# Folded-sum blocks as eight tiles, with gate and wide output products taken in column parts, in a Fourier-mixing and gated-feed-forward kernel

## The chip, the core and the metric

The kernel runs on one core of a Trainium2 chip. The metric is the device time of one execution in microseconds (us), the median of several runs. A core has a matrix engine (TensorE, in the profile PE, with its weight loads as PEld), three engines for elementwise work (VectorE or DVE, ScalarE or ACT, GpSimd or POOL), and SyncE (SP), which issues DMA transfers. TensorE writes to PSUM, eight banks of 512 float32 values for each of 128 partitions.

## The reference

```python
X = np.fft.fft(x, axis=1)          # x: (8, 3008, 256) float32
X = np.fft.fft(X, axis=2)
x = X.real.reshape(8 * 3008, 256)
gate = 1.0 / (1.0 + np.exp(-(x @ w_gate)))     # w_gate, w_val: (256, 1536)
val = x @ w_val
return gate * val @ w_out                      # w_out: (1536, 256)
```

Eight batches are transformed along the sequence and the features, the real part is kept, and each of the 24064 rows goes through a gated feed-forward layer.

## The kernel before, in words

Everything is float32. The symmetry of the transform lets the kernel compute sums over folded rows only, and the feature transform is merged into the gate and value weights (`merge`, line 411), so that three kinds of matrix products remain for each batch.

**The folded sums.** `quarter(b, blk)` (line 621) computes, for batch `b` from 1 to 7 and `blk` 1 then 0, a block of 48 products: 2 (`what`) x 2 (`part`) x 3 (`q`) x 4 (`TILES`, four groups of 32 partitions). Each has 31 or 32 contraction rows, 128 output columns of weights and 95 streamed columns, so it fills a quarter of the array's rows and the four of a round can run side by side, each into a PSUM bank of its own. Line 636 is the switch: for a (b, blk) in `HALVED` (line 78), each product is made as two, with 64 columns of weights each, so that eight tiles of 32 x 64 stand side by side. Before, seven of the fourteen blocks are in `HALVED`: (1, 0), (2, 0), (3, 1), (4, 1), (4, 0), (5, 0), (6, 1). Batch 0 is summed otherwise (`half`, line 596).

**The gate and value products.** The frequencies of a batch are cut into six chunks of 252 (the last of 246), and each chunk has 12 slices of 128 of the 1536 hidden features. An iteration `i` of the main loop (line 1153) is one such slice; there are 576, 72 to a batch. Its products are `front_a(i)` (two products, tile `pf` from `pk`) and `front_b(i)` (line 791; two products, `g` = 0 and 1, tile `pf` from `qk`), 252 columns each.

**The output products.** `back(p, part)` (line 859) multiplies the gated features by the output weights. From the second chunk on, an iteration makes 5 of the 15 products in `PRODUCTS` (line 67), 168 columns each. For the first chunk of batch 0 it takes the plain form of lines 866 to 882: two products of 504 columns for each of the 12 slices, 24 in all.

A float32 product is two passes of TensorE, and each pass is a weight load and a matmul: the page counts 12508 of each, and the program 6254 products. All products are issued through the helper `mm` at line 134, so all have that line in the profile; they are told apart by their tiles (`sum`, `pf`, `po`).

**The order of the work** is written out by hand. Each engine executes its instructions in the order in which the loop issues them. `mid` (line 1095 and line 1144) says in which iterations a block stands: block (b, blk) is issued in iteration (b - 1) x 72 + (4 - blk) x 12 + 5, and 12 later for b = 1, after that iteration's output products and before its `front_b`. Batches 2 to 7 issue transfers between partitions (`swap`, line 541) some iterations ahead of their blocks. ScalarE takes the four banks of a block away (line 646).

**The place of a block.** TensorE's instructions come to it by a DMA queue of their own, in packets of 16384 bytes. Over the program that is one packet for each 256 instructions. A block's place, in what follows, is the number of TensorE instructions ahead of it in the program, modulo 256, with four for each product and one for each separate wait. Before, the seven blocks in `HALVED` have the places 0, 248, 47, 228, 34, 215 and 14 (in order of time), the other seven 130, 122, 109, 89, 76, 195 and 65.

Of the kernel before, what the change touches and what calls it, by code (L numbers as in the profile page):

```python
# [74 lines left out]
          (12, 12, 11, 1), (13, 13, 6, 1), (7, 7, 10, 0), (5, 5, 7, 1))  # L75
C_LAST = (14, 9, 14, 0)
OUT = (3, 12)
HALVED = ((1, 0), (2, 0), (3, 1), (4, 1), (4, 0), (5, 0), (6, 1))
HUGE = float((2 ** 24 - 1 - 2 ** 20) * 2.0 ** -7)


# [1 line left out]
def kernel(  # L83
# [19 lines left out]
    NFT = F // P  # L103
# [28 lines left out]

    def mm(o, l, r, start, stop):
        nc.tensor.matmul(o, l, r, start=start, stop=stop, skip_group_check=True)  # L134

    def bank(name, other=None):
        if other is not None:
            return pso.tile([P, 512], F32, name=name, tag=f"po{other}")
        return psx.tile([P, 512], F32, name=name, tag="x")
# [43 lines left out]
    G2 = const.tile([P, 2, F], F32, name="G2")  # L183
# [227 lines left out]
    def merge(ws, g, c, other):  # L411
        cs = slice(c * WC, (c + 1) * WC)
        ps = bank("ps", other)
        for h in range(2):
            for t in range(2):
                mm(ps[:, h * WC : (h + 1) * WC], dt[:, t, h * HD : (h + 1) * HD], ws[:, t, :],
                   h == 0 and t == 0, t == 1)
        nc.scalar.copy(G2[:, g, cs], ps[:, WC : 2 * WC])
        nc.scalar.copy(G1[:, g, cs], ps[:, 0:WC])
        for f in range(c * WC // P, (c + 1) * WC // P):  # L420
            nc.sync.dma_start(
                out=ge[:, g, f : f + 1], in_=G2[0:1, g, f * P : (f + 1) * P])
# [173 lines left out]
    def half(b, w, d, blk, sn, other=None):  # L596


        c0, n = ((0, NE), (NE, NO))[blk]
        ev, od = [bank(name, other and other[i])[:, 0:n] for i, name in enumerate(("ev", "od"))]  # L600

        def sums(*qs):
            for q in sorted(qs, key=lambda q: q % 2):
                mm((ev, od)[q % 2], w(q), ST[int(sn)][0:NP, q, c0 : c0 + n], q < 2, q >= NQ - 2)

        def then():
            a = evp.tile([P, NE], F32, name="a", tag="a")[:, 0:n]
            nc.scalar.copy(a, ev)
            return lambda: places(d, blk, sn, a, od)
        return sums, then  # L610
# [10 lines left out]
    def quarter(b, blk):  # L621

        ps = [bank("sum", t + 1) for t in range(4)]
        for what in range(2):
            for part in range(2):
                for q in range(N3):
                    for t, (g, par, lo) in enumerate(TILES):
# [7 lines left out]
                        c0 = (2 * what + 1 - part) * NQ4  # L635
                        for at_ in (slice(0, HP), slice(HP, P)) if (b, blk) in HALVED else (slice(0, P),):
                            mm(ps[t][at_, c0 : c0 + NQ4], W[b, blk][what][rows, w, at_], tab,
# [111 lines left out]
    H, SF, EK = {}, {}, {}  # L749

    def cut(i):
        b, c, _ = groups[i // 3]
        k0, n = chunks[c]
        f = i % NFT
        return PQE[b], slice(k0, k0 + n), n, f, slice(f * P, (f + 1) * P)
# [8 lines left out]
    PF, AP, Z = {}, {}, {}  # L764
# [26 lines left out]
    def front_b(i):  # L791
        (_, qk, *_), ks, _, _, fs = cut(i)
        for g in range(2):
            mm(PF[i][:, g], G2[:, g, fs], qk[:, ks], False, True)

    def gate_a(i):

# [8 lines left out]
    def block(p, i):  # L806

        R = 2 * chunks[groups[p][1]][1] // 3
        return H[p][:, i % 3, i // 3 * R : (i // 3 + 1) * R] if i < 9 else SF[p][:, i - 9, 0:R]
# [19 lines left out]
    PO = []  # L829
# [3 lines left out]
    def rows_back(p, part):  # L833

        b, c, g = groups[p]
        k0, n = chunks[c]
        more = k0 + n > NK
        low, high = min(n, M - k0), n - more
        tiles = [(P, low - P, b * S + k0 + P), (n + more + P, high - P, b * S + S - k0 - n + 1 + more + P),
                 (0, P, b * S + k0), (n + more, P, b * S + S - k0 - n + 1 + more)]  # L840
        f0 = 3 * g + part
        if f0 == 0:
            PO[:] = [bank(f"po{t}", t) for t in range(4)]
            C[0] = cp.tile([P, 10 * WC], F32, name="c", tag="c")
        if g == NG - 1 and part < 2:
            return
        for t, (at_, m, r0) in enumerate(tiles):
            ps = PO[t][0:m, 0:D]
            for fh in (range(3) if g == NG - 1 else (part,)):
                f = 3 * g + fh  # L850
                mm(ps, H[p][:, fh, at_ : at_ + m], WL[0][:, f], f == 0, f == NFT - 1)
            if g == NG - 1:
                o = C[0][0:m, t * D : (t + 1) * D]
                (nc.vector.tensor_copy, nc.scalar.copy)[t % 2](o, ps)
                (nc.sync, nc.scalar)[t % 2].dma_start(out=out[r0 : r0 + m], in_=o)
        if part == 2:
            del H[p]

    def back(p, part):

        if p >= len(groups) - NG:
            return rows_back(p, part)
        b, c, g = groups[p]
        n = chunks[c][1]
        R = 2 * n // 3
        if p < NG:
            f = 3 * g + part
            if f == 0:
                PO[:] = [bank(f"po{t}", t) for t in range(2)]
            w = WO[f // 2].rearrange("p f (m h) -> p f h m", h=2)[:, f % 2]  # L870
            for h in range(2):
                mm(PO[h][:, 0 : 2 * n], w[:, h], H[p][:, part], f == 0, f == NFT - 1)
            if part == 2:
                del H[p]
            if f == NFT - 1:
                C[0] = cp.tile([P, 10 * WC], F32, name="c", tag="c")
                for x in OUT:
                    nc.gpsimd.memset(C[0][:, (x + 3) * R : (x + 3) * R + 40], 0.0)
                for h, copy in enumerate((nc.scalar.copy, nc.vector.tensor_copy)):
                    copy(C[0][:, OUT[h] * R : (OUT[h] + 3) * R], PO[h][:, 0 : 2 * n])  # L880
                finish(b, c, True)
            return
        if part == 0 and g == 0:
            PO[:] = [pso.tile([P, 2 * WC], F32, name=f"po{t}", tag=f"po{t}") for t in range(NB)]
        for at_, (hb, wb) in list(enumerate(PRODUCTS))[part * 5 : part * 5 + 5]:
            t, j = divmod(PLACE[at_], 3)
            mm(PO[t][:, j * R : (j + 1) * R], wf[:, g, wb], block(p, hb), g == 0 and at_ % 3 == 0,
               g == NG - 1)
            if g == NG - 1 and at_ % 3 == 2:
                if t == 0:  # L890
                    C[0] = cp.tile([P, 10 * WC], F32, name="c", tag="c")
                    nc.gpsimd.memset(C[0][:, 15 * R : 15 * R + 40], 0.0)
                (nc.vector.tensor_copy if t == 1 or t == 3 else nc.scalar.copy)(  # L893
                    C[0][:, 3 * t * R : 3 * (t + 1) * R], PO[t][:, 0 : 3 * R])
        if part == 2:
            del H[p], SF[p]
            if g == NG - 1:
                finish(b, c)
# [119 lines left out]

    per = NFT * len(chunks)
    side, mid, gap, spare = {}, {}, {}, {}  # L1020

    def at(i, *fs):
        side.setdefault(i, []).extend(fs)
# [129 lines left out]
    for i in range(count):  # L1153
# [11 lines left out]
        if i + 1 in mid:  # L1165
            back((i - 5) // 3, (i - 5) % 3)
        n = 3 if i >= count - 8 else 2 + (i % 2 and i not in (3 * i0 + 7, 3 * i0 + 9))
# [12 lines left out]
        if i >= 5 and i + 1 not in mid:  # L1180
            back((i - 5) // 3, (i - 5) % 3)
        merges = use.pop(i, [])
        for f in merges[0 : min(i, 1)]:
            f()
        front_b(i)
        for f in merges[min(i, 1) :]:
            f()
# [9 lines left out]
    for i in range(count, count + 5):  # L1197
        back((i - 5) // 3, (i - 5) % 3)
# [49 lines left out]
```

## Time and profile before

| | |
|---|---|
| median of 3 runs | 1907.24 us (1907.17 to 1909.02) |
| the profiled execution's own time | 1906.5 us |
| its span, first to last instruction | 1904.7 us |
| TensorE busy | 1894.5 us, 12508 passes |
| VectorE, ScalarE, GpSimd busy | 1518.6, 1353.0, 1544.1 us |
| granted TensorE clock | 1.00 throughout |

Busy time is the union of an engine's instructions. Matmuls overlap (a pass of 252 columns is shown as 376 ns long, while the next one starts 213 ns later), so what a pass costs is read from the distance between starts, not from its length. The chain of waits follows the work that ended last back from the end of the program: where it names an engine, shortening that engine's work there shortens the program, as long as nothing else comes to be last.

### The profile page before, as it was taken

Reading aid. Unit: us, or ns where it says so; the run is one execution under the profiler, and the core shown is the slowest. Engines: PE = TensorE matmul, PEld = TensorE weight load, DVE = VectorE, ACT = ScalarE, POOL = GpSimd, SP = SyncE. Lnnn points to the kernel's source line nnn. Section 1 sums busy time; section 2 is a strip of 40 time slices with the busy share of each in tenths; the row PEclk is TensorE's granted clock in tenths of the full one; section 3 lists DMA queues with packets and bytes.
Section 4 is the critical chain, followed back from the end, with each engine's and each line's share of the span. In section 5 each row is a group of like instructions: output and inputs, shape, how many; then the busy total and the mean of one; then the engine's idle time right before and its main releaser. Section 6 shows DMA issues by size and latency. Waiting matters only on the chain.

```text
span 1904.7 us, 37401 instructions
## 1 busy us (share of the span) xinstructions
PE 1894.5 (99%) x12508; PEld 1754.8 (92%) x12508; DVE 1518.6 (80%) x3375; ACT 1353.0 (71%) x3235; POOL 1544.1 (81%) x2733
## 2 busy tenths in 40 slices
PE   8999999999999999999999999999999999999999
PEld 5789999999999999999999999999999999999998
DVE  7678887878979778887788878887788777977775
ACT  4777777777777777777767777777777777777775
POOL 2389879987999879997799878999689986877770
PEclk9999999999999999999999999999999999999999
DMA  9346222212122121211211112112110110010001
GB/s 315 121 137 78 70 89 54 71 32 81 23 64 53 31 87 33 62 40 37 89 38 49 46 39 81 39 52 55 41 66 18 37 36 15 15 25 17 14 18 30
DMA packets 197338, 109.41 MB, mean 57 GB/s; under 512 B 134823, under 2 KB 188818, under 8 KB 195354
## 3 DMA queue, kind: packets, MB, share of 16 engines
q1 hardware_dynamic: 196568, 106.50, 21.1%
q8 instruction: 100, 1.64, 0.4%
q14 instruction: 92, 0.75, 0.1%
q10 hardware_dynamic: 546, 0.51, 0.1%
q0 software_dynamic: 32, 0.00, 0.0%
HBM read 71.24 MB, written 47.87 MB: 63 GB/s over the span
## 4 chain that ended last, share of the span: by engine, by line
PE 97%; POOL 1%; DMA 1%; DVE 0%; SPq 0%; ACT 0%; issue 0%; ACTq 0%; POOLq 0%
PE pf L134 51%; PE po L134 43%; PE sum L134 2%; PE ps L134 1%; POOL sf L826 1%; DMA st<-in_stab_dram 0%; DMA raw<-in_moe_w_val_dram 0%; PE od L134 0%; SPq L193 0%; POOL x L508 0%; SPq L376 0%; PE pe L134 0%; PE ev L134 0%; DVE c L910 0%; DVE z L804 0%
## 5 line engine op out<-in xcount | busy, mean ns | idle before, releaser
L826 POOL TENSOR_TENSOR sf<-h,sf 128x168 f32<-128x168 f32 (+1 forms) x1104 | 620.7, 582 | 76.0 <-DVE h L820 72.4
L826 POOL TENSOR_TENSOR sf<-h 128x168 f32<-128x168 f32 (+1 forms) x920 | 520.5, 585 | 160.1 <-DVE h L820 158.4
L134 PE MATMUL pf<-qk,G 128*128 128x252 f32 (+1 forms) x2304 | 583.5, 376 | 0.3 <-ACT ae L789 0.2
L134 PE MATMUL pf<-pk,G 128*128 128x252 f32 (+1 forms) x2304 | 582.9, 376 | 0.0
L774 ACT ACTIVATE pf<-ek,ge 128x252 f32<-128x252 f32 (+1 forms) x1142 | 538.2, 471 | 23.0 <-DMA ge<-G 3.2
L134 PE MATMUL po<-sf,wf 128*128 128x168 f32 (+1 forms) x2944 | 508.3, 305 | 0.0
L789 ACT ACTIVATE ae<-pf 128x504 f32<-128x504 f32 (+1 forms) x576 | 338.9, 588 | 218.1 <-PE pf L134 216.7
L134 PEld LDWEIGHTS pf<-pk,G 128*128 128x128 f32 x2304 | 435.8, 190 | 53.6 <-ACT pf L774 2.0
L134 PE MATMUL po<-h,wf 128*128 128x168 f32 (+2 forms) x2584 | 461.6, 307 | 0.0
L134 PEld LDWEIGHTS po<-sf,wf 128*128 128x128 f32 x2944 | 453.4, 190 | 8.0
L820 DVE TENSOR_TENSOR h<-pf,z 128x252 f32<-128x252 f32 (+1 forms) x576 | 240.4, 417 | 275.4 <-ACT pf L817 271.7
L804 DVE TENSOR_TENSOR z<-ae,pf 128x504 f32<-128x504 f32 (+1 forms) x576 | 384.5, 668 | 81.3 <-ACT h L803 77.3
L910 DVE TENSOR_TENSOR c<-c 128x168 f32<-128x168 f32 (+1 forms) x920 | 440.9, 503 | 3.3
L134 PEld LDWEIGHTS pf<-qk,G 128*128 128x128 f32 x2304 | 410.6, 190 | 31.6 <-issue 2.0
L134 PEld LDWEIGHTS po<-h,wf 128*128 128x128 f32 x2584 | 410.4, 190 | 18.1 <-issue 1.1
L803 ACT ACTIVATE h<-pf 128x252 f32<-128x252 f32 (+1 forms) x576 | 216.8, 376 | 146.4 <-PE pf L134 129.1
L817 ACT ACTIVATE pf<-z 128x252 f32<-128x252 f32 (+1 forms) x576 | 214.3, 372 | 119.0 <-DVE h L816 116.9
L816 DVE TENSOR_TENSOR h<-h,pf 128x252 f32<-128x252 f32 (+1 forms) x576 | 232.7, 404 | 0.0
L826 POOL TENSOR_TENSOR sf<-sf 128x168 f32<-128x168 f32 (+1 forms) x184 | 101.6, 552 | 14.4
L826 POOL TENSOR_TENSOR sf<-sf,h 128x168 f32<-128x168 f32 (+1 forms) x184 | 109.5, 595 | 0.0
L893 ACT COPY c<-po 128x504 f32<-128x504 f32 (+1 forms) x138 | 78.5, 569 | 0.0
L920 DVE STREAM_TRANSPOSE os<-c 128x256 f32<-128x256 f32 x188 | 76.5, 427 | 0.1
(158 smaller groups left out, 868.8 us busy)
## 6 DMA issues: line engine op xcount, KB each, us to landing
x<-xr SPq DMA_DIRECT2D x14, 1536.0 KB
out_dram<-os SPq DMA_DIRECT2D x376, 56.0 KB
xr<-in_xf_dram SPq DMA_DIRECT2D x105, 128.0 KB
x<-x SPq DMA_DIRECT2D x112, 96.0 KB
xr<-in_xf_dram SPq DMA_DIRECT2D x14, 384.0 KB
ek<-ed SPq DMA_DIRECT2D x40, 126.0 KB
out_dram<-os SPq DMA_DIRECT2D x288, 7.0 KB
xr<-in_xf_dram SPq DMA_DIRECT2D x21, 124.0 KB
```

What stands on the lines that cost most here:

```text
L134: nc.tensor.matmul(o, l, r, start=start, stop=stop, skip_group_check=True)
L774: nc.scalar.activation(PF[i][:, g], EK[i // NFT], AF.Copy, scale=ge[:, g, f : f + 1])
L789: nc.scalar.activation(AP[i], PF[i], AF.Copy, scale=2.0)
L803: nc.scalar.activation(H[p][:, fh, 0:n], PF[i][:, 0], AF.Sigmoid)
L804: nc.vector.tensor_tensor(z[:, :, ::-1], AP.pop(i), PF[i], op=ALU.subtract)
L816: nc.vector.tensor_tensor(h[:, fh, 0:n], h[:, fh, 0:n], pf[:, 1], op=ALU.mult)
L817: nc.scalar.activation(pf[:, 0], z[:, 0], AF.Sigmoid)
L820: nc.vector.tensor_tensor(h[:, fh, n:], pf[:, 0], z[:, 1], op=ALU.mult)
L826: nc.gpsimd.tensor_tensor(block(p, dst), block(p, a), block(p, b), op=(ALU.subtract, ALU.add)[op])
L893: (nc.vector.tensor_copy if t == 1 or t == 3 else nc.scalar.copy)(C[0][:, 3 * t * R : 3 * (t + 1) * R], PO[t][:, 0 : 3 * R])
L910: nc.vector.tensor_tensor(t[:, dst * R : (dst + 1) * R], *v, op=(ALU.subtract, ALU.add)[op])
L920: nc.vector.transpose(os_[0][0][:, s, 0:nb, h, :], t[:, c0 : c0 + nb * TB])
```

## The change

All fourteen blocks are put in `HALVED`. A new helper, `parts_mm`, makes a product as `n` products of adjoining columns, each with the same weights; only the first may start the accumulation in the bank. `front_b` uses it with two parts for its second product (`g` = 1) in 186 iterations: in the `n` iterations ahead of a block that `PARTED` names, for nine of the blocks. The 24 wide products of the first chunk are made in two parts of 252 columns, the last five in three parts of 168.

```diff
-HALVED = ((1, 0), (2, 0), (3, 1), (4, 1), (4, 0), (5, 0), (6, 1))
+HALVED = ((1, 1), (1, 0), (2, 1), (2, 0), (3, 1), (3, 0), (4, 1), (4, 0), (5, 1), (5, 0), (6, 1), (6, 0), (7, 1), (7, 0))
+PARTED = {(2, 1): 15, (2, 0): 1, (3, 1): 31, (3, 0): 1, (4, 1): 33, (4, 0): 1, (5, 1): 38, (6, 1): 31, (7, 1): 35}
+THIRDS = 5
...
+    def parts_mm(n, o, l, r, start, stop):
+
+        w = o.shape[1]
+        for k in range(n):
+            at_ = slice(k * w // n, (k + 1) * w // n)
+            mm(o[:, at_], l, r[:, at_], start and k == 0, stop)
...
     def front_b(i):
...
-            mm(PF[i][:, g], G2[:, g, fs], qk[:, ks], False, True)
+            parts_mm(2 if g and i in parted else 1, PF[i][:, g], G2[:, g, fs], qk[:, ks], False, True)
...
             for h in range(2):
-                mm(PO[h][:, 0 : 2 * n], w[:, h], H[p][:, part], f == 0, f == NFT - 1)
+                parts_mm(3 if 2 * f + h >= 2 * NFT - THIRDS else 2, PO[h][:, 0 : 2 * n], w[:, h], H[p][:, part],
+                         f == 0, f == NFT - 1)
...
+    parted = {(b - 1) * per + (4 - blk + (b == 1)) * NFT + 4 - k for (b, blk), n in PARTED.items() for k in range(n)}
+    assert len(parted) == sum(PARTED.values())
```

The program then has 6805 products in place of 6254: 336 more in the seven blocks, 186 more gate products and 29 more output products. The other engines have the same instructions in the same order. The places of the fourteen blocks become, in order of time, 246, 52, 233, 43, 220, 30, 215, 25, 229, 35, 212, 18, 211 and 17.

## The prediction

> **What bounds the kernel now.** I read the page's busy times and its chain of waits first, to see which engine a saving has to come from.
>
> ```profile
> PE 1894.5 (99%) x12508; PEld 1754.8 (92%) x12508; DVE 1518.6 (80%) x3375; ACT 1353.0 (71%) x3235; POOL 1544.1 (81%) x2733
> ...
> PE 97%; POOL 1%; DMA 1%; DVE 0%; SPq 0%; ACT 0%; issue 0%; ACTq 0%; POOLq 0%
> PE pf L134 51%; PE po L134 43%; PE sum L134 2%; PE ps L134 1%; POOL sf L826 1%; DMA st<-in_stab_dram 0%; DMA raw<-in_moe_w_val_dram 0%; PE od L134 0%; SPq L193 0%; POOL x L508 0%; SPq L376 0%; PE pe L134 0%; PE ev L134 0%; DVE c L910 0%; DVE z L804 0%
> ```
>
> TensorE is 97% of the chain, and the folded sums are only 2% of it. Busy time alone would not prove the bound, since passes overlap, so I also compared starts. The median distance between the starts of successive passes is 213 ns for 252 columns, 143 for 168, 139 for 164 and 423 for 504: within 0.7 ns, 0.833 ns a column and 3 ns a pass. Over the whole trace the distances exceed this line by 2.5 us in the first 48 us and by 0.6 us at most in any later slice of 48 us. So TensorE streams columns without a gap, and what is taken from it or added to it shows one to one in the end. After the first 33 us, most of which go to transfers, the chain leaves TensorE twice for longer than 0.2 us, at 318.9 to 351.8 us (GpSimd, VectorE) and at 1620.8 to 1625.5 us (ScalarE), but both detours begin at a TensorE pass, so a shift ahead of them is passed on.
>
> Next the chain in narrow windows, which gives the price of one block in each form. The columns are start, length and number of passes on the chain. A block of four tiles:
>
> ```profile
> 1603.52 1.70 PE pf L134 x8
> 1605.22 2.86 PE sum L134 x96
> 1608.09 1.62 PE po L134 x10
> ```
>
> and one of eight tiles, block (2, 0), with the dearest of its kind, (6, 1), behind it:
>
> ```profile
> 452.14 1.70 PE pf L134 x8
> 453.84 2.53 PE sum L134 x141
> 456.38 1.62 PE po L134 x10
> ```
>
> ```profile
> 1332.54 1.70 PE pf L134 x8
> 1334.24 2.63 PE sum L134 x151
> 1336.87 1.20 PE po L134 x7
> ```
>
> The neighbours cost the same in all three (eight gate passes 1.70), so the block's own length is the whole difference: 2.86 against 2.53 us. All seven four-tile blocks read 2.86. Of the seven eight-tile ones five read 2.53 or 2.54, (4, 1) reads 2.58 and (6, 1) 2.63.
>
> **The change part by part.**
>
> **Blocks as eight tiles.** Seven blocks go from 2.86 to 2.53: 7 x 0.33 = 2.3 us less. Each issues 48 products more, and nothing waits for them but ScalarE's four copies, as before. Bounds for a new eight-tile block are the rows 2.53 and 2.63: a gain of 1.6 to 2.3.
>
> One rule of the Trainium skill speaks against this step: "TensorEngine Tiling (Array Packing)", section Instruction Overhead, gives each matmul a floor of some 60 cycles however few its columns, and warns against tiling too finely. At 2.4 GHz that is an estimated 25 ns, so 192 passes would take 4.8 us and seven blocks would lose 14 us. The row above disagrees: 2.53 us over 192 passes is 13 ns each.
>
> **Their places.** The change's column parts move the blocks. Places that gave 2.53 or 2.54 before are 215, 248, 0, 34 and 47. The two dear blocks stood at 228 and 14, in between, so by these seven rows place alone does not order the lengths. What else differs is the DMA traffic (the last two columns are the share of the DMA engines and GB/s):
>
> ```profile
> 453.70:456.90 3.20, 2.60 (x192) 2.42 (x192) 0.62 (x3) 1.00 0.04 8
> 873.90:877.10 3.20, 2.65 (x192) 2.47 (x192) 0.64 (x4) 1.00 0.44 98
> 1334.10:1337.30 3.20, 2.70 (x192) 2.51 (x192) 0.59 (x3) 1.00 0.54 119
> ```
>
> The dear ones are (4, 1) at 0.44 and (6, 1) at 0.54; (3, 1) at 0.21 has 2.54, the rest at most 0.11. The new places, 211 to 246 and 17 to 52, lie inside or within five of the range tried. If place was the cause, 0.15 us come back; if it is DMA, (4, 1) and (6, 1) stay as they are and block (1, 1), with a share of 0.46 in the same view, comes out some 0.07 short of its 0.33. I take 0 here, with -0.15 to +0.1 as its bounds.
>
> **Wide output products.** A product is two passes. Two parts of 252 in place of 504 cost 2 x (2 x 213 - 423) = 6 ns, 19 times; three parts of 168 cost 2 x (3 x 143 - 423) = 12 ns, 5 times. Together 0.2 us more. Rows for both widths exist, and the chain is TensorE's there.
>
> **Gate products in parts.** This is the open price: no full-width pass of 126 columns is in the trace. By the line above it takes 105 + 3 = 108 ns, so a product costs 4 x 108 - 2 x 213 = 6 ns more, and 186 of them 1.1 us. That is the floor of a pass, so the lower bound, and it holds only if the weights of the next pass, 128 columns each time, are loaded in that time. The trace shows two rows that limit this from above. The narrowest full-width pass, 164 columns, starts every 139 ns, still on the line, so a load takes no longer; that gives 4 x 139 - 426 = 130 ns and 24 us. Nearer is the four-tile block: there a round of four tiles loads the same 128 columns and streams only 95, which by the line need 82 ns. It takes 2.86 us / 24 = 119 ns with both ends of the block counted, and 111.7 ns between rounds inside it, by the starts of its loads and passes. So loading 128 columns, not streaming, sets the pace there, at about 112 ns: 4 x 112 - 426 = 22 ns, 4.1 us in all. But in that block a load starts some 30 ns after the pass ahead of it, behind the other three tiles' passes. In full-width rows it starts 2 ns after. The first two loads of a tile stand 108 ns apart. I therefore take 108 for the load too, as the nearest row without that queue, and 1.1 us as the price.
>
> The Trainium skill has a figure for this: "TensorE: Matmul & The Clock Gate", section LDWEIGHTS, gives a load its number of columns divided by 1.2 in ns, 107 for 128. By it the load hides under the 108 by a hair and the sum is the same; the 112 of the block is 5 ns above it, and no run shows it for the full array.
>
> Nothing but TensorE's stream is touched: the other engines' order is unchanged, and the end of a gate product moves by nanoseconds. The instruction queue fetches some nine packets more (the page's 100 carry 1.64 MB at 0.4% of the DMA engines).
>
> **Sum**, against the profiled execution's own 1906.5 us: -2.3 + 0 + 0.2 + 1.1 = -1.0, so 1905.5. The median of the runs shown is 0.7 higher, 1907.24. On it the forecast is **1906.2 us**. A difference of 0.2%, 3.8 us, is about what a measurement of this kernel can tell from no change (its three runs span 1.9), so this is a forecast of no visible difference.
>
> **Rivals.**
>
> *Weight loads pace the parts, at the inner rate of the four-tile block.* At 112 ns the parts cost 4.1 instead of 1.1, the sum is +2.0 and the time 1909.2, still within 0.2%. For it: that block is paced by loads of this width. Against it: its queue of four tiles.
>
> *The same, dearer: slower than before.* With the whole 119 ns of the block's round, parts cost 4 x 119 - 426 = 50 ns, 9.3 us in all; the sum is +7.2 and the time 1914.4. The point from which it is slower by over 0.2% is (3.8 + 2.1) us / 186 = 32 ns a product, a pass of 114.4 ns. For it: nothing full-width in the trace is quicker than 139. Against it: 119 counts the block's ends.
>
> *Bad places.* All fourteen blocks at the dearest length seen: 14 x 2.63 = 36.8, against 7 x 2.86 + 5 x 2.53 + 2.58 + 2.63 = 37.9 now. The gain is 1.1, the sum +0.2, the time 1907.4. A place that costs more than seen needs 0.4 us a block to reach 0.2%.
>
> *The change does not do what it says*, new blocks staying at 2.86: 1908.5. Seven rows of exactly this kind of block speak against it.
>
> *All parts free and both dear blocks cured:* -2.3 - 0.15 + 0.2 = -2.3, and 1904.9; the line's 3 ns a pass speaks against it.
>
> **Chances.** Forecast 0.57, loads at 112 ns 0.17, dear loads 0.07, bad places 0.10, not as it says 0.02, parts free 0.07. Slower by over 0.2% is the dear loads plus a little for a place worse than any seen: 0.08. Faster by over 0.2% needs 3.8 us where all blocks together can give 2.5: 0.03. Within 0.2%: 0.89. The range for 8 in 10 takes in parts free, the forecast, bad places and loads at 112 ns: 1904.8 to 1909.2.
>
> **What the profile after would show.** In the chain, fourteen blocks at 2.53 to 2.63 and none at 2.86. In the timeline, gate groups of six passes ahead of a block, with the next group 0.86 us behind (0.87 if loads take 112 ns, 0.90 if 119). In the first chunk, wide groups 1.70 us apart where it was 1.69. I would be wrong if a part's second pass started later than 110 ns after its first, or if a new block showed a stall of tenths of a microsecond.

## The result and the profile after

The changed kernel takes 1913.01 us (median of 8 runs, 1911.59 to 1913.57), the kernel before on the same chip 1907.13: a ratio of 1.0029, with a 95% interval of 1.0019 to 1.0038. It is slower by 0.3%, outside the forecast range. The profiled execution takes 1913.41 us, 6.9 more than the one of before; the span grows by the same 6.9. The forecast sum was -1.0.

From the page of the kernel after (the first line is the span, then the busy times, the instruction queue and the chain of waits):

```profile
span 1911.6 us, 39593 instructions
...
PE 1897.3 (99%) x13610; PEld 1775.3 (93%) x13610; DVE 1524.3 (80%) x3375; ACT 1356.5 (71%) x3235; POOL 1545.2 (81%) x2733
...
q8 instruction: 109, 1.79, 0.4%
...
PE 96%; POOL 1%; DMA 1%; DVE 0%; ACT 0%; SPq 0%; issue 0%; ACTq 0%; POOLq 0%
```

TensorE still carries the chain, at full clock, with 1102 passes and 9 instruction packets more. Its busy time grew by only 2.8 us; in the other 4.1 us of the longer span the profile shows it idle, and the page's percentages hide that. So I compared, pass by pass, the distance from each start to the next start with that of before. The loss stands in few places:

| Part | forecast | measured (us) |
|---|---|---|
| 186 gate products in parts | +1.1 | +4.1 |
| fourteen blocks, first start to the start of the next work | -2.3 | +1.5 |
| other stops of TensorE: one of 0.89, 14 instructions behind block (1, 0), less small differences | 0 | +0.7 |
| wide output products | +0.2 | +0.1 |
| start of the program, end, small differences | 0 | +0.5 |

**The gate parts.** TensorE's timeline ahead of block (6, 1), with start, length as shown, and count of passes:

```profile
1335.39 1.59 PE L136 MATMUL po<-sf,wf 128*128 128x168 f32 x10
1336.81 1.03 PE L136 MATMUL pf<-qk,G 128*128 128x252 f32 x6
1337.68 0.59 PE L136 MATMUL pf<-pk,G 128*128 128x252 f32 x2
```

The row of six is two passes of 252 columns and four of 126 (the row names the form of its first). From its start to the next row's it takes 0.87 us, the figure that the prediction gave to loads at 112 ns. By starts, the first 126-column pass is followed after 107.5 ns, the other three after 111.7, and the 252-column pass behind them takes 216.7 instead of 212.5. With those 4.2 ns that is 446.8 against 425.0 ns for the product: 21.8 ns, 186 times.

**The blocks.** The chain of waits around block (2, 0), and then around block (6, 1):

```profile
453.27 1.72 PE pf L136 x10
455.00 2.53 PE sum L136 x136
457.53 1.48 PE po L136 x9
```

```profile
1336.98 1.72 PE pf L136 x10
1338.70 1.64 PE sum L136 x90
1340.33 1.05 issue
1341.38 1.20 PE sum L136 x62
1342.59 1.62 PE po L136 x10
```

In each of these rows the block stands ahead of its own iteration's output products, which follow it as `po`. Block (2, 0) has the price foreseen, 2.53 us, and so have eight others; (3, 1) has 2.54. Block (6, 1) is cut in two by a piece named "issue", time in which TensorE waited for nothing that the profile shows, and takes 3.89 us. (The piece counts from the end of a pass, which the profile models; from start to start the stop is 1.29 us.) Block (7, 1) takes 3.89 too, (4, 1) 3.55 and (1, 1) 2.76. The three long ones, (4, 1), (6, 1) and (7, 1), stop once, after 117, 119 and 119 of their 192 passes, and always at the same kind of instruction: number 194 modulo 256 in the program, counted as the places are. I take this to be where a new instruction packet begins, and call such a point a *packet boundary*.

The trace has the packets of TensorE's queue themselves, and the five blocks of the kernel after with places from 211 to 229 show what separates them (times from the block's first pass, in us; a stop is the distance between two starts):

```
block   place  packet starts  takes  block stops for  goes on at
(3, 1)  220    -3.34          1.51   -
(5, 1)  229    -2.83          1.22   -
(4, 1)  215    -0.24          1.19   0.95             2.40
(7, 1)  211    +0.02          1.43   1.29             2.75
(6, 1)  212    +0.50          0.94   1.29             2.75
```

Where the packet started late, the block stopped, and went on 1.3 to 1.5 us after the packet's end (start plus what it takes). The stop behind block (1, 0) ends in the same way, 1.46 us after the end of its packet, though the chain names ScalarE's copies there; the kernel before has the same copies and no stop. My theory from here: an eight-tile block issues 256 instructions in 1.7 us, and the next packet isn't there by then. The rival: the long blocks come from their batch or from the data traffic beside them, and the boundary is a coincidence; or, for the gate parts, from something other than the weight load.

### The profile page after: what moved, and what is told of

It reads as the page before. It is cut to its first block, busy times and chain, and to the rows that moved or that the text cites. A ratio compares the mean times of both kernels' runs of the same rounds, so it can differ in the third digit from the quotient of the medians.

```text
span 1911.6 us, 39593 instructions
## 1 busy us (share of the span) xinstructions
PE 1897.3 (99%) x13610; PEld 1775.3 (93%) x13610; DVE 1524.3 (80%) x3375; ACT 1356.5 (71%) x3235; POOL 1545.2 (81%) x2733
## 4 chain that ended last, share of the span: by engine, by line
PE 96%; POOL 1%; DMA 1%; DVE 0%; ACT 0%; SPq 0%; issue 0%; ACTq 0%; POOLq 0%
PE pf L136 51%; PE po L136 42%; PE sum L136 2%; PE ps L136 1%; POOL sf L835 1%; DMA st<-in_stab_dram 0%; DMA raw<-in_moe_w_val_dram 0%; PE od L136 0%; POOL x L517 0%; SPq L202 0%; SPq L385 0%; PE pe L136 0%; PE ev L136 0%; DVE c L920 0%; DVE z L813 0%
## 5 line engine op out<-in xcount | busy, mean ns | idle before, releaser
L136 PE MATMUL pf<-qk,G 128*128 128x252 f32 (+2 forms) x2676 | 586.9, 348 | 0.3 <-ACT ae L798 0.2
L136 PEld LDWEIGHTS pf<-qk,G 128*128 128x128 f32 x2676 | 451.9, 190 | 28.4 <-ACT ae L798 1.0
L136 PEld LDWEIGHTS pf<-pk,G 128*128 128x128 f32 x2304 | 421.8, 190 | 44.8 <-ACT pf L783 1.6
```

## The experiments

Ten kernels ran. "Before" beside each is a run of the kernel before on the same chip.

### Column parts alone

The kernel before, its seven `HALVED` blocks kept and at about their places, with 195 gate products in two parts.

```diff
-            mm(PF[i][:, g], G2[:, g, fs], qk[:, ks], False, True)
+            n = 2 if i % 72 < 32 + g and i // 72 in (3, 4, 5) else 1
+            for k in range(n):
+                w = PF[i].shape[2]
+                at_ = slice(k * w // n, (k + 1) * w // n)
+                mm(PF[i][:, g, at_], G2[:, g, fs], qk[:, ks][:, at_], False, True)
```

> The kernel before, with 195 gate products in two parts of 126 columns and nothing else; 65 of them stand ahead of each of the blocks (4, 1), (5, 1) and (6, 1), 65 x 4 instructions less four waits saved, so that all blocks keep their places to within 4 instructions. If a part is paced by streaming, 108 ns a pass, 195 x 6 ns = 1.2 us more than before. If it is paced by the weight load, at the 110.3 ns a pass (and 111.7 for the last) that the changed kernel shows, 195 x 16.6 ns = 3.2 us more. The block lengths stay as they were.

Measured: ratio 1.0020 (1.0011 to 1.0029), span 1908.8 us, 4.1 more; the blocks' sum is unchanged, 37.9 us. Its timeline shows eight passes of 126 columns in 0.89 us where four of 252 take 0.85:

```profile
791.75 1.05 PE L134 MATMUL pf<-qk,G 128*128 128x126 f32 x8
792.64 1.02 PE L134 MATMUL pf<-pk,G 128*128 128x252 f32 x4
```

By starts the first pass is followed after 107.4 ns, the next ones after 111.7, and the pass behind the row is again 4.2 ns longer: 21.6 ns a product, 4.2 us, where 16.6 ns and 3.2 us were expected. The price is that of the parts alone.

### Parts of 84 columns

The same with three parts for 192 products (`n = 3`), to tell a load that sets the pace from a fixed addition to each pass.

> The kernel before, with 192 gate products in three parts of 84 columns, 64 ahead of each of (4, 1), (5, 1) and (6, 1), places kept to within 7. If streaming paces a narrow pass, 84 columns take 73 ns and a product 6 x 73 - 425 = 13 ns more, 2.5 us in all, about 1909.4. If the weight load of 128 columns does, at 111.7 ns whatever the columns, it is 107.5 + 5 x 111.7 + 4 - 425 = 245 ns more, 47 us in all, about 1954.

Measured in one execution: 1953.02 us, span 1951.2, 46.5 more than before, some 242 ns a product.

```profile
790.26 1.46 PE L134 MATMUL pf<-qk,G 128*128 128x84 f32 x12
791.56 1.05 PE L134 MATMUL pf<-pk,G 128*128 128x252 f32 x4
```

Twelve passes of 84 columns take 1.30 us, and the 252-column pass behind them 252 ns instead of 212.5. The first is followed after 72 ns, which is its streaming (0.833 x 84 + 3 = 73, as the 107.5 were that of 126 columns); all others start 111.7 ns apart, the same as with 126 columns. So the pace is set by what the two have in common, a load of 128 columns of weights, and only the first pass of a row finds its successor's weights loaded already. That it is the number of weight columns is not shown further: no run loads fewer of them over the full height for passes this narrow. By the two lines, 0.833 ns a column + 3 and 111.7, a pass of fewer than about 130 columns costs the full load; that is an estimate.

### Fourteen blocks, no parts

The kernel after without `PARTED` and `THIRDS`: places as they fall, 130, 192, 58, 120, 175, 237, 36, 98, 153, 215, 14, 76, 131 and 193.

> All fourteen blocks as eight tiles, no product in parts. The places are, in order of time, 130, 192, 58, 120, 175, 237, 36, 98, 153, 215, 14, 76, 131 and 193. Theory of the fetch (a packet of instructions is asked for when TensorE's sequencer enters the packet ahead of it, comes about 3.4 us later, and packets begin at places near 194): a block that begins at a place of 66 to 194 runs through a whole packet, 1.7 us, before the next is there, and stands still for about 1.7 us. Nine blocks do, and one at 58 stands still right behind its end for about 1.2 us; 16 to 17 us lost against 2.3 gained, about 1921.5 us. Rival: the place is no cause, and the long blocks of the changed kernel come from transfers or from the parts ahead of them: seven blocks 0.33 us shorter, nothing added, about 1905 us.

Measured: 1919.80 us, ratio 1.0067 (1.0054 to 1.0080), span 1917.0 us. The seven blocks at the places from 76 to 175 took 3.41 to 4.58 us; the seven others 2.53 or 2.54. Block (1, 1), at 130, in the chain:

```profile
218.84 0.85 PE pf L134 x4
219.69 2.17 PE sum L134 x127
221.85 1.82 issue
223.68 0.59 PE sum L134 x32
```

At 130 the boundaries stand at instructions 64 and 320 of the block's 384, with 1.7 us between them, and the second packet, which started 1.70 us behind the block's first pass, was not there in time. The kernel before has four-tile blocks at 130, 122, 109, 89, 76 and 65 without a gap: 192 instructions in 2.86 us never hold two boundaries. Blocks (1, 0) and (7, 0), at 192 and 193, were expected long and were short: their packets had started 1.0 and 1.2 us ahead of them. Block (2, 1), at 58, is short, but two passes just behind it, where its second boundary falls, start 1.14 us apart.

### The three long blocks moved

The kernel after with 4 parts more ahead of (4, 1) and (6, 1) and 4 fewer ahead of (5, 1), which moves (4, 1), (6, 1) and (7, 1) from 215, 212 and 211 to 231, 229 and 228.

> The changed kernel with four more parts ahead of (4, 1), four fewer ahead of (5, 1), four more ahead of (6, 1), so that the blocks (4, 1), (6, 1) and (7, 1) move from places 215, 212 and 211 to 231, 229 and 228; the number of parts grows by four in all. Theory of the fetch: the three read 2.53 to 2.6 us in place of 3.55, 3.89 and 3.89, and the time falls by 3.7 us, to about 1909.3. Rival (transfers, or the parts themselves): they stay long and the time stays at 1913.

Measured: 1911.51 us, ratio 1.0022 (1.0013 to 1.0031), span 1908.9 us in the profiled execution. (4, 1) went from 3.55 to 2.53 and (6, 1) from 3.89 to 2.55, so the batch alone isn't the cause. But (7, 1), at 228, took 3.62: its packet started 0.16 us ahead of it, where that of (6, 1), one place further on, started at -3.10. The place sets what a late packet costs, and something else whether it is late.

### All blocks at 230 and 36, by no-ops

No parts; instructions without an operation in TensorE's stream, up to four in an iteration, bring each blk 1 to 230 and each blk 0 to 36.

```diff
+        for _ in range(pads.get(i, 0)):
+            nc.tensor.nop("pad", nofuse=True)
```

> All fourteen blocks as eight tiles, no product in parts, and 867 no-op instructions of TensorE spread over the iterations, four to an iteration, in 35 or fewer ahead of a block, so that every blk 1 stands at place 230 and every blk 0 at 36. Theory of the fetch: all fourteen read 2.53 to 2.63 us, as the no-ops cost the array nothing while its queue has work; 2.3 us less than before, about 1904.8. If a no-op stops the queue, 867 times its cost is added (10 ns each: 8.7 us). Rival to the fetch: some blocks stay at 3 us or more wherever they stand.

Measured, with 867 no-ops: ratio 0.9990 (0.9981 to 0.9998). Thirteen blocks take 2.53 or 2.54 us, (1, 1) takes 2.75; the sum is 35.7, against 37.9 before. With batch 1 left as it was before, and 803 no-ops:

> As the kernel with no-ops, but batch 1 is left as it was before ((1, 1) as four tiles, no no-ops ahead of its blocks); 803 no-ops put the blocks of batches 2 to 7 at places 230 and 36. Theory of the fetch: twelve eight-tile blocks at 2.53 to 2.55 us and (1, 0) at 2.53; six blocks 0.33 us shorter and the two dear ones of before some 0.1 less, 2.1 us less than before, about 1904.7. If the no-ops themselves cost something, the gain is smaller here as it was there.

Measured: 1904.01 us, ratio **0.9986** (0.9977 to 0.9995), span 1902.3 us. Block (6, 1), long in the kernel after, in the chain of this one:

```profile
1331.31 1.70 PE pf L135 x8
1333.01 2.53 PE sum L135 x154
1335.54 1.62 PE po L135 x10
```

This is the fastest version of the study and beats both kernels. The blocks give back 2.1 us and the span 2.4: eight hundred no-ops, four to an iteration and none within 20 passes behind a block, cost nothing that can be seen, where the 186 column parts of the change cost 4.1.

### The stretch from 206 to 226

With no-ops as in the last kernel, the blk 1 blocks of batches 2 to 7 at 226, 222, 218, 214, 210 and 206; then the other way round.

> As the kernel before this one, with the blk 1 blocks of batches 2 to 7 at places 226, 222, 218, 214, 210 and 206 in order of time (and blk 0 at 32 down to 12). If the place alone decides, the first blocks read 2.53 us and from an edge near 215 on they read 3.5 to 3.9. If the batch decides (its transfers), the same batches as in the changed kernel are long, 4, 6 and 7, and 5 is short.

> The same places given to the batches in the opposite order: 206, 210, 214, 218, 222 and 226 for batches 2 to 7. If the place alone decides, now batches 2, 3 and perhaps 4 are long and 5 to 7 short; if the batch decides, the picture of the run before this one repeats. If neither, the lateness of a packet has a part that varies by itself, and the long ones agree with the packets that begin late, not with place or batch.

Measured in one execution each. Falling places: 2.54, 3.42, 3.44, 3.62, 3.73, 2.54 us (span 1906.3). Rising, 206 to 226: 2.53, 2.56, 2.84, 2.57, 2.54, 2.53 (span 1903.2). Place 210 gives 3.73 in one and 2.56 in the other. In this stretch neither place nor batch decides; the packet's start does, again: each block over 3.4 us has one between -0.48 and +0.03 us, each under 2.6 has one at -1.2 or earlier.

### The stretch with and without transfers beside it

Every blk 1 of batches 2 to 7 at 214, with every blk 0 at 20; then every blk 0 at 214, with every blk 1 at 40. In these two the no-ops stand up to 16 to an iteration, not four.

> Thirteen blocks of eight tiles, batch 1 as before, no column parts, 787 no-ops: every blk 1 of batches 2 to 7 at place 214, in the stretch of places where a block was long in one execution and short in another, and every blk 0 at place 20, where none was. The blk 1 blocks have the transfers between partitions beside them (a DMA share of 0.65 to 0.8 in the 3 us ahead of them), the blk 0 blocks hardly any. Theory A (a packet of instructions waits behind those transfers): about half of the six blk 1 blocks are long, 3.4 to 3.9 us, as eight of eleven such were until now, so 3 to 5 us more than the version with no block in that stretch (1904.0): 1907 to 1909. Theory B (the stretch alone, whatever the transfers): the same here.

> The same the other way round: every blk 0 of batches 2 to 7 at place 214, and every blk 1 at 40; 981 no-ops. Theory A (packets wait behind the transfers): no blk 0 block is long, since little is transferred ahead of it; packets start 1 to 3 us ahead of each; 1904.0 to 1905. Theory B (the stretch alone): as many long blocks as in the other kernel, 1907 to 1909.

Measured: 1906.35 and 1910.56 us, ratios 1.0000 (0.9991 to 1.0009) and 1.0019 (1.0009 to 1.0028); both miss their expectations. With blk 1 at 214 the time scatters from 1903.8 to 1909.4 us (11 runs; before 1905.8 to 1907.6), and in the profiled execution two of six are long, 3.02. With blk 0 at 214 none is: five take 2.53 or 2.54 and one 2.75, and their packets start at -1.3 and -0.8. Two of six against none of six is a thin difference by itself.

The second kernel's total misses for another reason: behind each of its six blk 1 blocks TensorE stops for 0.7 to 1.4 us, 6.5 us in all. Two things stand there: the boundary that place 40 puts 26 instructions behind the block, and three instructions further the 16 no-ops of the next iteration. Behind block (6, 1):

```profile
1341.65 0.59 PE L135 MATMUL pf<-qk,G 128*128 128x252 f32 x2
1342.43 0.58 PE L135 MATMUL pf<-qk,G 128*128 128x252 f32 x2 [0.19 <-issue]
1343.76 1.09 PE L135 MATMUL pf<-pk,G 128*128 128x252 f32 x4 [0.75 <-issue]
```

The first "issue" is at the boundary; such delays are 0.9 us in all six places together. The second lies over the no-ops: in the trace they start 71 ns apart, 16 of them 1.2 us from the first to the last, and the next pass starts 0.07 us behind the last. These are the other 5.6 us. The 51 other groups of 16 in this kernel, away from the blocks, delay TensorE by 0.07 us at most. So, by these rows, no-ops cost nothing only where TensorE has work queued for as long as they take; right behind a block and a boundary it had not. The fastest version has its blk 0 blocks at 36, the boundary 30 instructions behind them, no no-ops there and no stop.

The DMA share, slice by slice ahead of two blk 1 blocks of the first kernel, both at 214. First (3, 1), long, which starts at 644.38 us, then (4, 1), short, at 875.21 (window, length, TensorE, clock, DMA share, GB/s):

```profile
641.40:642.40 1.00, 1.00 (x9) 1.00 0.72 164
642.40:643.40 1.00, 1.00 (x7) 1.00 0.62 143
643.40:644.40 1.00, 1.00 (x9) 1.00 0.76 168
```

```profile
872.20:873.20 1.00, 1.00 (x9) 1.00 0.59 131
873.20:874.20 1.00, 1.00 (x7) 1.00 0.50 111
874.20:875.20 1.00, 1.00 (x6) 1.00 0.74 163
```

and ahead of block (3, 0) of the second kernel, at 685.27 us, the three us together:

```profile
682.30:685.30 3.00, 3.00 (x22) 1.00 0.03 5
```

Block (4, 1) has a pause in the transfers in its middle slice, block (3, 1) none, block (3, 0) no transfers to speak of. Over all kernels, 29 eight-tile blk 1 blocks stood between 206 and 229; 11 took 2.84 us or more, the others at most 2.58. For all 11, every slice of the four us ahead of the block has a share of 0.58 or more. Of the 18 short ones, 15 have a slice of 0.55 or less in the last two us, and the other three one of at most 0.22 in the first us of the block. Of nine blk 0 blocks between 214 and 217, none was longer than 2.75. That fits a packet that waits behind the transfers until they pause; it is an association, with bounds drawn after the fact, and not shown by an intervention on one block. Nor can the transfers be all: ahead of those nine, with hardly any in the three us before, the packet started at -3.0 once, at -0.8 once and near -1.3 in the others.

## Why the prediction was wrong, step by step

**Blocks as eight tiles, -0.33 us each: right**, where no packet is late. Thirteen at 2.53 or 2.54 in one kernel show it, and the blocks' sum falls by 2.1 to 2.3 us. (A block has eight copies of ScalarE behind it, not four, 112 for fourteen blocks; nothing hangs on that.)

**Gate parts: the term was mis-sized.** The step that failed is "I therefore take 108 for the load too, as the nearest row without that queue". It took the distance of the first two loads of a tile for the pace of a row of loads. The runs show the inner rate of the four-tile block, 111.7 ns, to the tenth, in rows of full-height loads that have no queue of four tiles. The rival "weight loads pace the parts" had this term exactly, 22 ns and 4.1 us. The Trainium skill's figure was on the wrong side: by "TensorE: Matmul & The Clock Gate", section LDWEIGHTS, a load of 128 columns takes 107 ns; in the traces loads that follow each other start 111.7 apart. The 107.5 of the first step is no load but the streaming of 126 columns, as the 72 with 84 columns show. My first sign to watch was badly aimed too: a part's second pass did start 107.5 ns after its first; the third tells. The other sign, a stall of tenths of a microsecond in a new block, did show.

**Places: the step that failed** is "lie inside or within five of the range tried", and with it "I take 0 here, with -0.15 to +0.1 as its bounds". It read five lengths at five places as if each place had one length. What decides is whether the next packet is there when TensorE comes to the boundary. Seventeen blocks have a stop inside them, in five kernels (the kernel after, the one without parts, the shifted one, the falling places and blk 1 at 214): each stop is at a boundary, and each block goes on 1.2 to 1.6 us after the end of that boundary's packet. The place sets where in the block the boundary lies, and so how much work there is from the boundary ahead of it: 2.9 to 3.3 us in the long blocks of the kernel after, at 211 to 215, 4.1 at 228, 1.7 at 130. With 1.7 us and boundaries inside the block, as at 130, the stop was 2.06 us. With 4.1 us most blocks near 230 had none, but (7, 1) at 228, whose packet started late, stopped for 1.0. At 215 and 220 the packet sometimes starts early, as for (5, 0) before and (3, 1) after, and one sample of each looks safe. The trace of before held a sign: behind (3, 1), at 47, one step takes 253 ns instead of 143, at a boundary. The queue's 0.4% of the DMA engines, which I did read, says how much it carries and not when a packet comes. The Trainium skill, "Runtime: NRT & Kernel Launch", section Instruction fetch mechanics, calls the cost of such a boundary mostly hidden; that agrees with every four-tile block, none of which stops, and the stops of 0.4 to 2.1 us of the eight-tile ones speak against it.

**The rival "bad places"** had the mechanism's place but not its price: it took the dearest length seen, 2.63. Its point of decision, 0.4 us a block over all fourteen, was reached by three blocks alone, which lost 3.7 us between them beside a fast one.

**Wide products: right**, 0.1 against 0.2 us. **The bound: right**; the gaps and the parts add up to the span's 6.9 us but for 0.5. Without late packets the sum is -2.3 + 4.1 + 0.1 = +1.9, within 0.2%; of the 5.0 us that are left, 3.8 stand in the blocks and 0.7 in stops outside them, and these make it slower.

**Open:** what holds a packet back (the transfers are the likely cause, on the rows above), what else lets it start earlier or later, and the small lengthenings of 0.05 to 0.25 us, as of (1, 1) at 246 and at 230, which neither the place nor the DMA share orders.

## What to carry to other kernels

Before instructions are made smaller and more numerous on the engine that bounds the kernel, count how many it will issue in the time that one instruction packet needs to come: here 256 in some 4 us or less can open a gap at a packet boundary, and the profile calls it "issue". Where a dense block must stand well to the boundaries, move it by no-ops and not by splitting products. No-ops cost nothing here when spread four to an iteration; 16 in a row right behind a block held TensorE up for 0.7 to 1.0 us. Splitting costs a full weight load, 111.7 ns for 128 columns, as soon as the pass streams for less. Put it where both boundaries leave room, not where one execution happened to be short: compare several blocks at each place, with and without transfers beside them.

## What the runs showed that was not expected

After the longest gaps TensorE runs at half its clock for a while. Behind (1, 1) of the fourteen blocks without parts, whose gap is 2.06 us, nine passes of 168 columns started 269 to 280 ns apart instead of 143. The same followed a gap of 1.96 us, and not one of 1.94. TensorE's timeline there, and the granted clock in slices of 1 us (the number behind the count of passes):

```profile
220.77 1.09 PE L134 MATMUL sum<-st,x 31*64 31x95 f32 x68
223.68 0.59 PE L134 MATMUL sum<-st,x 32*64 32x95 f32 x32 [1.82 <-issue]
224.19 2.12 PE L134 MATMUL po<-h,wf 128*128 128x168 f32 x7
```

```profile
223.00:224.00 1.00, 0.33 (x28) 1.00 1.07 343
224.00:225.00 1.00, 1.00 (x31) 0.72 0.99 259
225.00:226.00 1.00, 1.00 (x5) 0.50 0.95 210
226.00:227.00 1.00, 1.00 (x6) 0.50 0.66 138
```

Seven passes fill 2.12 us in the row before the slices; at 143 ns between starts they would take about 1.2. The trace has the granted clock at 0.50 for 3.4 us behind each of the two gaps, from 224.4 and from 924.2 us, and at 1.00 around them. So behind a gap of 2 us another 1.6 to 1.7 us are lost. These few gaps don't give the rule by which the clock falls.
